# Leaving out 50 of the 125 idle matrix products among the first attention units

## The chip, the cores and the metric

The kernel runs on one core of one Trainium2 chip. The metric is the time of one execution on the device in microseconds (us). The engines are PE (TensorE, matrix products; PEld is its weight load), DVE (VectorE), ACT (ScalarE), POOL (GpSimd) and SP (SyncE, which issues transfers). Each takes its own instructions strictly in the order in which the program has them, and waits at one until what that one needs is there.

## The reference

A recurrent attention (4 batches, 8 heads, 768 steps, head size 48) gives 3072 tokens of width 384. Two expert layers follow: a dense one with a gated activation and a layer norm, and one that sends each token to one of 8 experts.

```
for t in range(S):                         # attention, per batch and head
    cur   = (u * k[t]) outer v[t]
    y[t]  = r[t] @ (state + cur)
    state = w[t][:, None] * state + k[t] outer v[t]
h  = x @ w_in                              # first layer, 3072 x 1024
ln = layernorm(h * softmax(h)) * g_ln
x2 = ln @ w_out
e  = argmax(x2 @ w_gate)                   # second layer
out = gate * (relu(x2 @ w1[e]) @ w2[e])
```

## The kernel before, in words

The attention is cut into 24 units: 6 chunks of 128 steps for each of 4 batches, all 8 heads at once. For a unit, PE turns w, r and k with its transposes (L686, tiles lw, lr, lk); DVE makes running products of the decay (L700, tile qe); ACT and POOL make their reciprocals (L710, L712 on ACT; L717, L721, L722 on POOL, tile tq); DVE forms kt (L727) and rt (L705). PE multiplies kt by rt (L762, the scores); DVE copies the masked scores into am (L766); PE forms the unit's output (L780), turns kt back (L795) and forms the state's update (L807, from ks, which ACT copies at L800). ACT and DVE split each output into a high and a low part (L785, L788).

The first 7 units run without any product of the expert layers beside them. In that time the weights of the first layer, which arrive as 64-bit numbers, are also put together with bit operations on DVE (L226 to L229) and split on ACT and POOL, and PE turns the output weights for the gate (L256, L263). This part takes some 81 us of the run. From then on each attention unit is emitted together with a unit of the first layer (products of L186 to L189), and at the end come the 8 experts.

The order of all of this is written down. Every step is entered in a plan with a planned time by `at(t, fn)`. `emit` sorts the plan by that time and then calls the steps in the order of a fixed list of 2000 numbers, `_ORDER`. So a step keeps its place as long as the number of steps and their planned times stay as they are.

The idle products are eight such steps. `WARM` holds pairs of a count and a planned time, and each pair becomes one step that issues that many products of a 128x128 block of ones with itself, in bfloat16, into a corner of a PSUM bank that nobody reads:

```
WARM = (28, -213.38, 17, 35.27, 40, -60.18, 7, -131.3, 21, 14.69, 0, 23.63, 11, 143.22, 1, 178.42)

def warm(n):
    for _ in range(n):
        nc.tensor.matmul(flat(0)[:, DM:512], ones16, ones16, start=True, stop=True)

for n, t in zip(WARM[0::2], WARM[1::2]):
    at(min(t, t_step[LAG] - 2.0), lambda n=n: warm(n))
```

The planned times are numbers of the plan and no times of the chip. One of the eight counts is 0 already: such a step stands in the plan and issues nothing.

Of the kernel before, what the change touches and what calls it, by code (L numbers as in the profile page):

```python
# [119 lines left out]
def rwkv_moe_kernel(ctx: ExitStack, tc: tile.TileContext, r, k, v, w, u, w_in, w_out, g_ln, w_gate, w1, w2, out, dbg=None):  # L120
# [480 lines left out]
    def at(t, fn):  # L601
        plan.append((t, len(plan), fn))
# [60 lines left out]
    }  # L663
    TAIL0 = 4.0
    STEP = {'po': 56.09, 'pi': 84.42, 'mix': 15.94, 'last': 19.69, 'tail': 8.58}
    WARM = (28, -213.38, 17, 35.27, 40, -60.18, 7, -131.3, 21, 14.69, 0, 23.63, 11, 143.22, 1, 178.42)
    mode_of = lambda s: "po" if s < 3 else "pi" if s < LAG else "mix" if s < NU - 1 else "last" if s == NU - 1 else "tail"
    t_step = {-1: 0.0}
    for s in range(-1, NU + LAG + 2):
# [411 lines left out]
# [6 lines that stand above are left out]
# [306 lines left out]
```

## Time and profile before

| what | us |
|---|---|
| median of 3 runs | 651.63 |
| lowest, highest of the 3 | 649.35, 655.84 |
| the profiled execution | 653.84 |
| its span, first to last instruction | 651.8 |
| PE busy in the span | 617.9 |

The mean granted clock of PE over the span is 0.981 of full speed. An execution's time is 2.0 us longer than its span. The profiled execution is one of several and lies 2.2 us above the median, within what the three runs span.

### The profile page before, as it was taken

How to read it: one execution, taken by the hardware profiler on the slowest of the kernel's cores; microseconds unless marked ns; L12 is line 12 of the kernel's file. 1: busy time of each engine (PE TensorE's matmuls, PEld its weight loads, DVE VectorE, ACT ScalarE, POOL GpSimd, SP SyncE). 2: the span in 40 equal slices, each digit the busy share in tenths (PEclk: the TensorE clock that was granted, in tenths of full speed). 3: DMA queues.
4: the chain of work that ended last, by engine and by line, in shares of the span. 5: the costliest groups of instructions: out<-in, count | busy, mean ns of one | idle time of the engine just before them, and what ended most of it. 6: DMA issues, size and time to landing. Idle time of an engine off the chain costs nothing. (4 is left out here: it accounts for less than half of the span.)

```text
span 651.8 us, 13454 instructions
## 1 busy us (share of the span) xinstructions
PE 617.9 (95%) x5143; PEld 562.8 (86%) x5143; DVE 355.0 (54%) x876; ACT 340.2 (52%) x711; POOL 369.0 (57%) x389
## 2 busy tenths in 40 slices
PE   5888899999999999999999999899999999999993
PEld 4767688888898888888888998898999999999993
DVE  8999967685767767868657675233212112121210
ACT  5577655564755646554547874245354335353420
POOL 7998896453485635466202344276467546566611
PEclk9789899999999999999999999899999999999997
DMA  8984414436443423511004401554445415535200
GB/s 210 239 215 115 99 20 87 114 106 189 135 117 67 99 50 74 103 34 38 13 1 121 147 25 50 194 180 143 145 142 195 153 56 179 168 113 184 73 34 26
DMA packets 125103, 72.56 MB, mean 111 GB/s; under 512 B 104071, under 2 KB 115836, under 8 KB 125029
## 3 DMA queue, kind: packets, MB, share of 16 engines
q1 hardware_dynamic: 121749, 62.13, 35.3%
q0 software_dynamic: 3280, 9.47, 3.9%
q8 instruction: 43, 0.70, 0.5%
q14 instruction: 31, 0.25, 0.1%
HBM read 55.79 MB, written 16.29 MB: 111 GB/s over the span
## 5 line engine op out<-in xcount | busy, mean ns | idle before, releaser
L1254 DVE SCALAR_TENSOR_TENSOR hl<-bank,hh 128x384 fp32r<-128x384 f32 (+5 forms) x70 | 37.0, 551 | 113.3 <-ACT hh L1253 103.8
L1047 POOL TENSOR_TENSOR wbl<-stg,wbh 128x768 fp32r<-128x768 f32 x32 | 58.8, 1852 | 27.7 <-ACT wbh L1046 25.5
L1253 ACT ACTIVATE hh<-bank 128x384 fp32r<-128x384 f32 (+5 forms) x70 | 33.0, 489 | 78.4 <-PE bank L189 63.8
L195 PE MATMUL bank<-wbh,hh 128*128 128x384 f32 (+4 forms) x216 | 73.9, 342 | 0.0
L195 PE MATMUL bank<-wbl,hh 128*128 128x384 f32 (+4 forms) x216 | 72.6, 336 | 0.0
L186 PE MATMUL bank<-xth,wah 128*128 128x384 f32 (+5 forms) x210 | 71.3, 344 | 0.6 <-ACT xth L1246 0.5
L187 PE MATMUL bank<-xtl,wah 128*128 128x384 f32 (+5 forms) x210 | 70.1, 339 | 0.2 <-DVE xtl L1247 0.2
L1047 POOL TENSOR_TENSOR wal<-stg,wah 128x1024 fp32r<-128x1024 f32 x24 | 57.4, 2402 | 20.9 <-ACT wah L1046 18.9
L186 PE MATMUL bank<-wbh,lh 128*128 128x392 f32 x192 | 67.7, 353 | 0.5 <-ACT hh L1253 0.5
L187 PE MATMUL bank<-wbl,lh 128*128 128x392 f32 x192 | 65.3, 340 | 0.0
L1273 POOL DMA_INDIRECT out_dram<-yo,xg x28 | 27.6, 985 | 58.2 <-ACT yo L1270 40.7
L717 POOL TENSOR_TENSOR tq<-qe,yq 128x512 f32<-128x512 f32 x24 | 29.9, 1244 | 51.0 <-ACT yq L712 39.1
L189 PE MATMUL bank<-xth,wal 128*128 128x384 f32 (+5 forms) x210 | 48.1, 338 | 0.0
L958 POOL DMA_INDIRECT xsd<-xo,ai x24 | 24.4, 1017 | 40.1 <-DMA xsd<-xo,ai 16.6
L395 DVE TENSOR_TENSOR ll<-bank,lh 128x512 fp32r<-128x512 f32 x48 | 32.6, 685 | 22.7 <-ACT lh L391 20.3
L186 PE MATMUL pair<-wah,wah 128*128 128x512 f32 x102 | 41.4, 406 | 1.2 <-DVE wbl L268 0.9
L195 PE MATMUL bank<-wbh,hl 128*128 128x384 f32 (+4 forms) x216 | 42.1, 336 | 0.0
L186 PEld LDWEIGHTS bank<-xth,wah 128*128 128x128 f32 x210 | 40.2, 191 | 2.2 <-ACT xth L1246 0.6
L187 PEld LDWEIGHTS bank<-xtl,wah 128*128 128x128 f32 x210 | 40.3, 192 | 1.4 <-DVE xtl L1247 0.4
L358 ACT ACTIVATE cc<-s,nmu 128x1024 f32<-128x1024 f32 x24 | 27.6, 1151 | 26.3 <-DVE nmu L356 25.6
L195 PEld LDWEIGHTS bank<-wbh,hh 128*128 128x128 f32 (+4 forms) x216 | 39.3, 182 | 0.9
L195 PEld LDWEIGHTS bank<-wbl,hh 128*128 128x128 f32 (+4 forms) x216 | 39.4, 182 | 0.8
(236 smaller groups left out, 1635.8 us busy)
## 6 DMA issues: line engine op xcount, KB each, us to landing
stg<-in_moe_w_dram SPq DMA_DIRECT2D x32, 384.0 KB, 3.1
stg<-in_moe_w_dram SPq DMA_DIRECT2D x24, 512.0 KB, 4.2
xsd<-zrow SPq DMA_DIRECT2D x16, 386.0 KB, 5.8
xg<-xsd SPq DMA_DIRECT2D x24, 193.0 KB, 3.1
lw<-in_w_dram SPq DMA_DIRECT2D x24, 192.0 KB, 3.8
lr<-in_r_dram SPq DMA_DIRECT2D x24, 192.0 KB, 4.2
lk<-in_k_dram SPq DMA_DIRECT2D x24, 192.0 KB, 2.9
lv<-in_v_dram SPq DMA_DIRECT2D x24, 192.0 KB, 2.6
```

Of the source, the lines that this page charges most:

```text
L186: nc.tensor.matmul(o, ah, bh, start=(i == 0), stop=False)
L187: nc.tensor.matmul(o, ah, bl, start=False, stop=False)
L189: nc.tensor.matmul(o, al, bh, start=False, stop=(i == n - 1))
L195: nc.tensor.matmul(o, a, b, start=(i == 0), stop=(i == len(seq) - 1))
L358: nc.scalar.activation(out=u["cc"], in_=u["s"], func=AF.Identity, bias=u["nmu"])
L395: yield 1.05 + 0.55 * g, lambda g=g, gs=gs: nc.vector.tensor_tensor(out=u["ll"][:, gs, :], in0=lp[g], in1=u["lh"][:, gs, :].bitcast(F32), ...
L717: nc.gpsimd.tensor_tensor(out=u["tq"], in0=u["qe"][:, :, 1:129], in1=u["yq"], op=ALU.mult)
L958: nc.gpsimd.indirect_dma_start(out=xsd, out_offset=bass.IndirectOffsetOnAxis(ap=u["ai"][:, j, :], axis=0), in_=MU[m]["xo"], in_offset=None ...
L1047: at(t + c1, lambda: eng.tensor_tensor(out=dl(), in0=u["st"], in1=dh().bitcast(F32), op=ALU.subtract))
L1253: at(t + d1, lambda: nc.scalar.activation(out=P2["h", 0][:, f, cs], in_=hp, func=AF.Relu))
L1254: at(t + d2, lambda: nc.vector.scalar_tensor_tensor(out=P2["h", 1][:, f, cs], in0=hp, scalar=0.0, in1=P2["h", 0][:, f, cs].bitcast(F32), o ...
L1273: nc.gpsimd.indirect_dma_start(out=out, out_offset=bass.IndirectOffsetOnAxis(ap=xg(j, i)[0:n, XW - 1:XW].bitcast(I32), axis=0), in_=box["y ...
```

## The change

Four of the eight counts are set to 0: those of 17, 21, 11 and 1 products. The groups of 28, 40 and 7, which are issued together at the start, stay.

```
-    WARM = (28, -213.38, 17, 35.27, 40, -60.18, 7, -131.3, 21, 14.69, 0, 23.63, 11, 143.22, 1, 178.42)
+    WARM = (28, -213.38, 0, 35.27, 40, -60.18, 7, -131.3, 0, 14.69, 0, 23.63, 0, 143.22, 0, 178.42)
```

The number of steps and their planned times are as before, so all other instructions keep their order. Without the idle products the list of PE's instructions is the same in both programs, and so are those of DVE, ACT, POOL and SP.

On PE, before, the group of 17 stands between a state update (L807) and the scores of a unit (L762). The sixteen further pairs of a weight load and a product are not shown:

```order
L795 MATMUL bank_160<-ident,kt 128x128 x4
L686 MATMUL bank_159<-ident,lw_165 128x128 x4
L256 MATMUL pair_158<-ident,wst 128x128 x6
L807 MATMUL bank_160<-lv_175,ks 64x48 x8
L1084 LDWEIGHTS ones_78
L1084 MATMUL pair_158<-ones_78 128x128
```

On PE, after, the scores follow the state update directly (bank_161 and bank_162 are the PSUM banks of the even and odd heads' scores):

```order
L795 MATMUL bank_160<-ident,kt 128x128 x4
L686 MATMUL bank_159<-ident,lw_165 128x128 x4
L256 MATMUL pair_158<-ident,wst 128x128 x6
L807 MATMUL bank_160<-lv_175,ks 64x48 x8
L762 MATMUL bank_161<-rt,kt 128x128
L762 MATMUL bank_162<-rt,kt 128x128
```

Nothing else moved here: the 34 rows are gone. The same holds at the single product, on PE some way further on, where the next instruction is a transpose of r:

```order
 L256 MATMUL pair_158<-ident,wst 128x128 x3
 L807 MATMUL bank_160<-lv_176,ks 64x48 x8
-L1084 LDWEIGHTS ones_78
-L1084 MATMUL pair_158<-ones_78 128x128
 L686 MATMUL bank_163<-ident,lr_169 128x128 x4
 L263 MATMUL pair_158<-wgt,wT 128x8 x3
```

The weight load and the product are gone, and the neighbours keep their places.

## Rows read from the trace of the kernel before

**Rows 1.** Busy time of each engine in two stretches (windows view).

```profile
core 0: us, PE busy (x) PEld busy (x) DVE busy (x) ACT busy (x) POOL busy (x), PEclk, DMA share, GB/s
3.55:81.00 77.45, 62.41 (x846) 53.54 (x846) 71.28 (x126) 52.84 (x126) 68.64 (x68) 0.91 0.76 180
81.00:641.00 560.00, 555.44 (x4298) 509.22 (x4298) 281.13 (x737) 285.62 (x585) 296.48 (x288) 1.00 0.35 104
```

**Rows 2.** The idle products of L1084: shortest, median, longest ns.

```profile
L1084 PE MATMUL pair<-ones x125: 216/219/314, 4.4 to 71.0; 128*128 128x128 bf16 x125
```

**Rows 3.** Timeline of PE: start, us, what, [idle before <- releaser].

```profile
20.32 1.35 PE L1084 MATMUL pair<-ones 128*128 128x128 bf16 x21
23.46 1.10 PE L807 MATMUL bank<-lv,ks 128*64 128x48 f32 x16 [1.80 <-ACT ks L800]
...
30.93 1.12 PE L1084 MATMUL pair<-ones 128*128 128x128 bf16 x17
31.98 1.16 PE L762 MATMUL bank<-rt,kt 48*128 48x128 f32 x16
```

**Rows 4.** Timeline of ACT at 21.7 to 23.4 us.

```profile
21.71 0.72 ACT L710 ACTIVATE yq<-qe,tiny 128x512 f32<-128x512 f32 x1 [4.35 <-POOL tq L722]
...
22.84 0.56 ACT L800 COPY ks<-bank 128x512 f32<-128x512 f32 x1
```

**Rows 5.** Timeline of DVE: all its rows with a wait from 18 to 77 us.

```profile
18.58 1.36 DVE L700 TENSOR_TENSOR_SCAN qe<-bank,zeros 128x128 f32<-128x128 f32 x4 [0.35 <-PE bank L686]
...
33.18 0.76 DVE L766 COPY_PREDICATED am<-causal,bank 128x512 f32<-128x512 int32 x1 [0.37 <-PE bank L762]
...
38.98 0.69 DVE L727 TENSOR_TENSOR kt<-bank,tq 128x512 f32<-128x512 f32 x1 [0.25 <-POOL tq L722]
...
47.69 1.37 DVE L700 TENSOR_TENSOR_SCAN qe<-bank,zeros 128x128 f32<-128x128 f32 x4 [0.82 <-PE bank L686]
...
55.97 1.38 DVE L766 COPY_PREDICATED am<-causal,bank 128x512 f32<-128x512 int32 x2 [0.57 <-PE bank L762]
...
76.53 1.37 DVE L766 COPY_PREDICATED am<-causal,bank 128x512 f32<-128x512 int32 x2 [0.82 <-PE bank L762]
```

**Rows 6.** Timeline of POOL: two rows with a wait, neighbours among its waits.

```profile
27.14 1.37 POOL L717 TENSOR_TENSOR tq<-qe,yq 128x512 f32<-128x512 f32 x1 [0.37 <-DVE kt L727]
...
51.55 1.45 POOL L717 TENSOR_TENSOR tq<-qe,yq 128x512 f32<-128x512 f32 x1 [1.36 <-ACT yq L712]
```

**Rows 7.** Timeline of PE, 60 to 81 us.

```profile
60.12 0.78 PE L1084 MATMUL pair<-ones 128*128 128x128 bf16 x11
...
63.45 0.66 PE L686 MATMUL bank<-ident,lr 128*128 128x128 f32 x4 [0.60 <-DVE rt L705]
...
73.10 0.66 PE L795 MATMUL bank<-ident,kt 128*128 128x128 f32 x4 [0.89 <-DVE su L815]
...
74.54 1.97 PE L762 MATMUL bank<-rt,kt 48*128 48x128 f32 x16 [0.35 <-DVE wal L788]
...
80.98 0.50 PE L186 MATMUL pair<-wah,wah 128*128 128x512 f32 x1 [0.91 <-DVE wbl L268]
```

**Rows 8.** Windows view by granted clock (PEclk, before the last two columns).

```profile
16.67:20.08 3.41, 3.41 (x24) 3.08 (x24) 2.77 (x8) 0.69 (x3) 3.41 (x4) 0.50 1.14 250
20.08:23.49 3.41, 1.61 (x29) 1.32 (x25) 3.28 (x5) 1.78 (x4) 3.33 (x4) 1.00 1.05 242
23.49:26.91 3.42, 3.42 (x48) 2.91 (x52) 3.32 (x5) 2.41 (x7) 3.13 (x4) 0.50 0.95 275
26.91:43.97 17.06, 13.65 (x199) 11.17 (x195) 16.30 (x33) 12.85 (x31) 16.11 (x17) 1.00 0.87 208
43.97:47.39 3.42, 3.42 (x28) 3.04 (x28) 2.90 (x4) 2.42 (x6) 3.25 (x4) 0.50 1.15 238
...
74.69:78.10 3.41, 3.41 (x44) 3.05 (x48) 2.59 (x4) 1.76 (x5) 3.41 (x4) 0.50 1.10 220
...
419.40:422.90 3.50, 3.48 (x16) 3.48 (x17) 0.00 (x0) 1.84 (x3) 1.19 (x1) 0.51 0.90 308
```

## The prediction

> **What bounds the kernel now.** I read the busy time by stretches first [rows 1]. From 81 to 641 us PE is busy 555.44 of 560 us at a granted clock of 1.00: here every microsecond that PE starts later ends the kernel later. From 3.55 to 81 us PE is busy only 62.41 of 77.45 us, DVE 71.28 and POOL 68.64. In this first part PE has slack, and DVE and POOL with their order of work set when the dense part can begin. The idle products all lie in it: the 125 of L1084 have a median of 219 ns each, and the last one starts at 71.0 us [rows 2]. The dense part begins at 80.98 us, when PE, after 0.91 us of waiting, gets what DVE made last (L268) [rows 7]. So the question is whether leaving out 50 products changes when DVE and POOL are done with the first part. Two ways lead there: PE's place in their waits, and PE's clock.
>
> **The change part by part: the time of the products.** Nothing else moves on any engine, so what can go is what the four groups take from PE. The 21 start at 20.32 and take 1.35 us. The 17 start at 30.93, and the scores behind them at 31.98: 1.05 us [rows 3]. The 11 take at most 0.78 us [rows 7], the single one at most 0.22 us [rows 2]. Together at most 3.4 us of PE.
>
> The 21: behind them PE sits idle for 1.80 us all the same, until ACT has copied ks at 23.40 [rows 3, 4]. ACT was late because it had waited 4.35 us, until 21.71, for POOL [rows 4]. Without the products the pause is longer and ends at the same moment. Value: 0.
>
> The 17: this is the group that somebody waits for. The scores end at 31.98 + 1.16 = 33.14, and DVE, idle for 0.37 us, starts its masked copy at 33.18 [rows 3, 5]. Without the group the scores can begin about 1.05 us earlier and DVE loses its wait. What is late next is POOL: DVE's next wait, 0.25 us at 38.98, ends with POOL's L722 [rows 5], and POOL has no wait between the two at 27.14 and 51.55 [rows 6], so it runs through without needing anything sooner. DVE's 0.37 us will come back as a wait of about 0.62 us at 38.98. Value: 0. The bound below is -0.37 us, if POOL too were helped by DVE's earlier work.
>
> The 11 and the single one: DVE has no wait between 55.97 and 76.53 [rows 5], so PE is not what it lacks there; PE itself waits 0.60 us for DVE's rt at 63.45 [rows 7]. Value: 0. For the single product I take 0 as well; the bound is its 0.22 us.
>
> **The clock.** Before, the granted clock was 0.50, which is the 1.2 GHz level, in four stretches of the first part and in one later, at 419.4 [rows 8]. Ahead of the stretch that begins at 23.49 PE had been busy for 1.61 of 3.41 us, with the 21 products among that: the group did not keep the clock up. Ahead of the one at 43.97 lay 17.06 us at full clock, of which PE was busy 13.65 us [rows 8], with the 17 early in it.
>
> What does a slow stretch cost? The same 16 products of L762 take 1.16 us at full clock [rows 3] and 1.97 us at half [rows 7]. What reaches the end is less, since PE has slack here. I take it from the waits of DVE for PE inside or right behind each stretch: 0.35 us at 18.58, none for the stretch at 23.49, 0.82 us at 47.69, 0.82 us at 76.53 [rows 5]. That is 1.99 us for four, 0.5 us each and at most 0.82. In the dense part there is no slack: PE was busy 3.48 us at 0.51 [rows 8], and half of that, 1.74 us, is the price of that stretch.
>
> The Trainium skill, "TensorE: Matmul & The Clock Gate", section "Terms", prices the time at the lower clock at that time multiplied by one minus the clock's ratio, here one half. By it the four stretches (13.66 us together) would cost 6.8 us, where DVE's waits show 1.99; in the dense part the rule and the row agree.
>
> How many stretches will there be without the 50? The 21 products were in vain, so there nothing changes. Around the 17 the pause of PE grows by what the scores move forward, less than 0.4 us in this first look: about 1.05 us earlier at the front, and the masked copy only 0.37 us earlier behind. Around the 11 the pause before 63.45 grows by at most 0.78 us. That makes at most 1.4 us, and less than the 1.80 us behind which the clock was low at 23.49 [rows 3, 8]. I expect the same number of slow stretches, perhaps shifted, and take 0; the bounds are one stretch fewer (-0.82) and one more in the dense part (+1.74).
>
> **The sum** against the profiled execution: 0 + 0 + 0 + 0 for the groups and 0 for the clock, 653.84 us as before, between -1.4 (-0.37 - 0.22 - 0.82) and +1.74 us. That execution is 2.2 us above the median of 651.63, a difference as large as any term here. I forecast the median unchanged, 651.6. Within 1% (6.5 us) is about what a measurement of this kernel can tell from no change.
>
> **Rivals.** First, faster: the products stood on the path after all, because the waits that the trace names are only those that ended last. Then all of their 3.4 us come back: 651.6 - 3.4 = 648.2. For it speaks DVE's 0.37 us at 33.18; against it the three other groups, behind which PE goes on waiting for others.
>
> Second, slower, by the clock. Without the groups of 17 and 11 the clock falls in more places of the first part, and each fall makes DVE wait for PE as at 47.69 and 76.53. Three more stretches at 0.82 us, and one that reaches over 81 us into the dense part at 1.74 us, make 4.2 us: 655.8. It decides where PE at half clock becomes what DVE waits for, which a unit's scores do: 1.97 instead of 1.16 us. For it speaks that four stretches were slow even with the products; against it that PE, once slow, is busy all the time (3.41 of 3.41 us) and the clock rose after each [rows 8], so that a fall does not stay.
>
> The Trainium skill's page "TensorE: Matmul & The Clock Gate", section "Why this matters for your kernels", warns against pauses of PE between bursts of products, since the clock then goes back to half: it speaks against this change. The trace agrees that it fell after pauses (behind the 1.80 us at 23.46), and shows that idle products in front of one did not prevent it. By the price of half the slow time that the Trainium skill gives, four more stretches would be 6.8 us and the time 658.4.
>
> Third, a different length of the stretch at 419.4, or none, by chance: 1.74 us either way, as executions differ anyway (649.35 to 655.84); this is part of the forecast's own spread.
>
> **How the numbers follow.** Forecast 0.70, first rival 0.12, second 0.18. The forecast's own range is the sum's bounds and the spread of the three runs, about 649 to 655. With the first rival at 648.2 and the second at 655.8 partly in, the range is 648.8 to 655.6. Faster by more than 1% (below 645.1) is more than all 50 products are worth: 0.02. Slower by more than 1% (above 658.1) needs eight further stretches at 0.82, or the second rival with two more falls in the dense part: 0.05. Within 1%: 0.93.
>
> **What the changed profile would show.** If I am right: the wait of DVE for L762 near 33.18 is gone, and that of DVE for POOL's L722 near 38.98 has grown to about 0.6 us; PE's wait for ks near 23.46 has grown from 1.80 to about 3.1 us; the dense part begins within 1 us of 80.98; the stretches at clock 0.50 are four or five before 81 us. I am wrong on the slow side if there are seven or more such stretches and DVE's waits for PE add up to over 5 us; on the fast side if the dense part begins before 79 us at the same clock.

## The result, and the profile after

| | before | after |
|---|---|---|
| median of 20 runs each, us | 652.52 | 656.94 |
| lowest, highest | 649.35, 658.51 | 654.92, 659.48 |
| the profiled execution, us | 653.84 | 658.72 |
| its span, us | 651.8 | 656.9 |
| mean granted clock of PE in it | 0.981 | 0.970 |

The kernel became slower: the ratio is 1.0064 with a 95% interval of 1.0048 to 1.008, some 4.2 us. That is less than 1%, and outside the forecast range. The instructions of all engines are the same but for the 50 products, so the time must lie in when things run. The windows view of the profile after, for the two stretches of [rows 1]:

```profile
3.55:81.00 77.45, 64.12 (x756) 55.19 (x759) 69.05 (x123) 51.70 (x123) 67.17 (x67) 0.82 0.73 176
81.00:641.00 560.00, 553.42 (x4321) 507.15 (x4313) 283.65 (x740) 285.68 (x585) 297.21 (x289) 0.99 0.36 104
```

In the first part PE is busy longer (64.12 us for 62.41) with 90 products fewer in the stretch (the 50, and others that now come after 81 us), and the granted clock has gone from 0.91 to 0.82. DVE and POOL got less done in it (69.05 for 71.28, 67.17 for 68.64): they waited. Where the clock is low shows in the windows view cut at its changes, to be held against [rows 8]:

```profile
16.08:19.49 3.41, 3.32 (x16) 2.99 (x18) 2.33 (x6) 1.29 (x5) 3.33 (x4) 0.50 0.99 201
19.49:22.91 3.42, 0.85 (x16) 0.66 (x12) 3.29 (x7) 1.11 (x2) 3.34 (x4) 1.00 1.09 244
22.91:39.98 17.07, 15.86 (x146) 13.02 (x147) 14.77 (x25) 11.50 (x30) 13.55 (x16) 0.50 0.70 181
39.98:46.80 6.82, 5.61 (x86) 4.76 (x88) 6.19 (x14) 4.61 (x11) 6.59 (x7) 1.00 0.96 222
46.80:50.21 3.41, 3.41 (x30) 3.02 (x19) 2.74 (x4) 2.72 (x7) 3.24 (x4) 0.50 1.01 224
422.27:429.10 6.83, 6.37 (x30) 5.96 (x30) 1.26 (x3) 3.22 (x5) 3.78 (x2) 0.50 0.68 224
```

Where before had 3.42 us at 0.50 from 23.49 and then 17.06 us at 1.00, after has 17.07 us at 0.50, though PE is busy in 15.86 of them. The timeline of PE, rows that answer to [rows 3, 7] and two more:

```profile
23.55 1.10 PE L807 MATMUL bank<-lv,ks 128*64 128x48 f32 x16 [3.21 <-ACT ks L800]
...
28.80 1.09 PE L795 MATMUL bank<-ident,kt 128*128 128x128 f32 x4
29.68 1.06 PE L686 MATMUL bank<-ident,lw 128*128 128x128 f32 x4
30.54 0.85 PE L256 MATMUL pair<-ident,wst 128*128 128x128 f32 x3
31.95 0.90 PE L256 MATMUL pair<-ident,wst 128*128 128x128 f32 x3 [0.57 <-ACT wT L259]
32.78 1.10 PE L807 MATMUL bank<-lv,ks 128*64 128x48 f32 x16
33.81 2.08 PE L762 MATMUL bank<-rt,kt 48*128 48x128 f32 x16
...
83.67 0.50 PE L186 MATMUL pair<-wah,wah 128*128 128x512 f32 x1 [0.93 <-DVE wbl L268]
...
420.90 0.55 PE L1244 MATMUL bank<-ident,xg 128*128 128x128 f32 x3 [2.63 <-DMA xg<-xsd]
```

The pause before ks ends at 23.55 (23.46 before), as it should without the 21. But the scores that began at 31.98 with the 17 products ahead of them begin at 33.81 without, and take 2.08 us instead of 1.16. The engines behind them, in the timelines of DVE, ACT and POOL (one fence, the same profile):

```profile
35.92 0.76 DVE L766 COPY_PREDICATED am<-causal,bank 128x512 f32<-128x512 int32 x1 [1.93 <-PE bank L762]
41.83 0.69 DVE L727 TENSOR_TENSOR kt<-bank,tq 128x512 f32<-128x512 f32 x1 [0.63 <-PE bank L686]
...
34.01 0.48 ACT L813 COPY su<-bank 128x384 f32<-128x384 f32 x1 [2.11 <-PE bank L807]
...
34.56 1.09 POOL L820 TENSOR_TENSOR St<-su,qe 64x192 f32<-64x192 f32 x2 [2.51 <-ACT su L813]
```

DVE's wait of 0.37 us at 33.18 [rows 5] has become 1.93 us at 35.92; POOL, which had no wait between 27.14 and 51.55 [rows 6], now waits 2.51 us for ACT, which waited 2.11 us for PE's L807. From 44 us on the first part is late by the same amount. Matching PE's instructions of the two traces one by one (start after minus start before): +0.15 us at 27, +2.66 at 44, +2.65 at 53, +2.68 where the dense part begins (83.67 for 80.98, worked out at its first rows), +2.19 at 412, +4.92 from 425 to the end. So there are **two places**: some 2.5 us arise between 27 and 44 us, about 0.5 us is regained in the dense part, and 2.73 us arise between 412 and 425 us, where the experts start. These figures belong to this pair of profiles, and profiles of one kernel differ (below).

At the second place PE waits for the rows gathered for the first expert: 2.63 us at 420.90 in after. In the profile before the same wait reads as follows (timeline of PE, not shown so far):

```profile
417.10 1.15 PE L1244 MATMUL bank<-ident,xg 128*128 128x128 f32 x6 [1.03 <-DMA xg<-xsd]
```

The gather is issued by SP, which waits for the last scatter of rows. SP's waits from 405 to 424 us, first after, then before:

```profile
SPq L1235 <- DMA xsd<-xo,ai: 4.1, 1, 4.1
```

```profile
SPq L1235 <- DMA xsd<-xo,ai: 2.3, 1, 2.3
```

The pause is 1.60 us longer, and behind it PE is busy 6.37 us at clock 0.50 where it was 3.48 before [rows 8]; half of that difference is 1.45 us. Together 3.05, of which 2.73 show in the starts.

### The profile page after: what moved, and what is told of

The parts are those of the page before. It is cut to its first block, busy times and chain, and to the rows that moved or that the text cites. A ratio compares the mean times of both kernels' runs of the same rounds, so it can differ in the third digit from the quotient of the medians.

```text
span 656.9 us, 13354 instructions
## 1 busy us (share of the span) xinstructions
PE 622.3 (95%) x5093; PEld 566.8 (86%) x5093; DVE 355.3 (54%) x876; ACT 339.8 (52%) x711; POOL 369.2 (56%) x389
## 5 line engine op out<-in xcount | busy, mean ns | idle before, releaser
L1047 POOL TENSOR_TENSOR wal<-stg,wah 128x1024 fp32r<-128x1024 f32 x24 | 57.2, 2397 | 22.0 <-ACT wah L1046 19.6
L717 POOL TENSOR_TENSOR tq<-qe,yq 128x512 f32<-128x512 f32 x24 | 30.1, 1254 | 50.1 <-ACT yq L712 35.3
L358 ACT ACTIVATE cc<-s,nmu 128x1024 f32<-128x1024 f32 x24 | 27.6, 1151 | 25.5 <-DVE nmu L356 25.4
L195 PEld LDWEIGHTS bank<-wbh,hh 128*128 128x128 f32 (+4 forms) x216 | 39.3, 182 | 0.9
```

The source lines that it names most:

```text
L195: nc.tensor.matmul(o, a, b, start=(i == 0), stop=(i == len(seq) - 1))
L358: nc.scalar.activation(out=u["cc"], in_=u["s"], func=AF.Identity, bias=u["nmu"])
L717: nc.gpsimd.tensor_tensor(out=u["tq"], in0=u["qe"][:, :, 1:129], in1=u["yq"], op=ALU.mult)
L1047: at(t + c1, lambda: eng.tensor_tensor(out=dl(), in0=u["st"], in1=dh().bitcast(F32), op=ALU.subtract))
```

## The experiments

Every kernel was compared with the kernel before on the same chip. The table has the ratio (95% interval) and what one profile of each shows: where the clock was 0.50, for stretches that begin between 13 and 45 us; the start of DVE's third masked copy of L766 (33.18 before); the first row of the dense part (80.98 before); PE's pause before the first gathered rows, near 417 us, and the time at 0.50 behind it (1.03 and 3.4 before). "None" stands for a pause that is no longer there; "ahead" for half clock that is over before this pause (410.9 to 414.3 us in no17, 409.8 to 413.2 in no11, behind another pause of 2.18 and 2.35 us). Each profile is one execution, and single executions differ. With "21" stand the kernels that issue 21 or more full products at 20 us.

| kernel | ratio | at 0.50, us | copy | dense | pause, 0.50 |
|---|---|---|---|---|---|
| before (21) | 1 | 16.7–20.1, 23.5–26.9, 44.0–47.4 | 33.18 | 80.98 | 1.03, 3.4 |
| look_before (21) | | 14.3–21.1 | 32.85 | 80.62 | 0.86, 0 |
| only21 (21) | 1.0022 (0.9998–1.0047) | 15.4–22.2, 35.8–39.3 | 32.84 | 79.76 | 1.16, 3.4 |
| no17 (21) | 1.0024 (0.9998–1.005) | 15.0–21.8, 35.4–42.3 | 32.84 | 81.83 | 1.25, 3.4 ahead |
| no11 (21) | 1.0025 (1.0005–1.0046) | 13.8–20.7 | 32.83 | 80.55 | 0.14, 3.4 ahead |
| one48 (21) | 1.0007 (0.9983–1.003) | 15.8–19.2, 36.2–39.7 | 32.83 | 79.75 | 0.63, 3.4 |
| fill21 (21) | 1.0014 (0.9992–1.0037) | 15.7–19.1, 29.3–32.7, 43.0–46.4 | 34.07 | 82.16 | 0.68, 0 |
| moved_with (21) | 1.0013 (0.999–1.0037) | 16.2–19.6, 36.7–40.1 | 32.87 | 82.51 | 0.68, 0 |
| late_with (21) | 0.9998 (0.9974–1.0022) | 15.7–19.1, 29.3–32.7, 43.0–49.8 | 34.08 | 81.35 | none, 0 |
| swap_with (21) | 0.999 (0.9969–1.001) | 16.1–19.5, 36.5–40.0, 43.4–46.8 | 32.83 | 82.38 | 0.42, 0 |
| both_with (21) | 1.0024 (0.9999–1.0049) | 16.1–19.5, 36.6–40.0, 43.4–46.8 | 32.86 | 82.47 | none, 0 |
| fillboth (21) | 1.0048 (1.0027–1.007) | 25.4–35.6 | 36.36 | 81.88 | 2.43, 6.8 |
| after | 1.0064 (1.0048–1.008) | 16.1–19.5, 22.9–40.0 | 35.92 | 83.67 | 2.63, 6.8 |
| look_after | | 15.1–39.0 | 35.91 | 82.22 | 2.73, 6.8 |
| no21 | 1.0057 (1.004–1.0075) | 14.7–35.2 | 36.70 | 84.50 | 1.30, 3.4 |
| tiny21 | 1.0028 (0.9999–1.0056) | 16.1–19.5, 22.9–36.5 | 37.30 | 82.84 | 2.69, 3.4 |
| moved_without | 1.0042 (1.0019–1.0064) | 14.9–35.3 | 34.75 | 82.36 | 2.69, 6.8 |
| late_without | 1.0036 (1.0017–1.0055) | 14.4–28.0, 38.3–41.7 | 34.63 | 81.76 | 1.45, 0 |
| swap_without | 1.0036 (1.001–1.0063) | 16.8–20.2, 23.6–27.0, 44.1–47.5 | 32.74 | 81.01 | 0.92, 3.4 |
| both_without | 1.0043 (1.0023–1.0063) | 16.6–20.0, 23.4–26.8, 43.9–47.3 | 32.73 | 81.46 | 0.08, 3.4 |

Two things hold over the whole table. First, in all runs and not only in the profiles, every kernel with the 21 has a higher mean granted clock (0.981 to 0.985) than every kernel without (0.973 to 0.978; 10 to 20 runs each). Second, matched to the profile of before, the profiles without the 21 are on average later than those with them by 1.1 us just behind the dense part's start (85 us), by 1.6 us at 405 and by 3.3 us at 425. So about half of the loss arises ahead of the experts' start and half there.

**The theory** after the result: without the 21 products PE's clock is at half when PE starts again behind the pause before ks, and stays there through the row of PE's work from 27 to 35 us on which DVE and POOL wait. **Its rivals**: the 17 or the 11, not the 21, carry the time; the products' place in PE's order matters and not their work; or the whole loss arises at the start of the experts.

### Which group carries the time

The edits are in the table of counts alone, against the kernel before.

```diff
-    WARM = (28, -213.38, 17, 35.27, 40, -60.18, 7, -131.3, 21, 14.69, 0, 23.63, 11, 143.22, 1, 178.42)
no21:
+    WARM = (28, -213.38, 17, 35.27, 40, -60.18, 7, -131.3, 0, 14.69, 0, 23.63, 11, 143.22, 1, 178.42)
only21:
+    WARM = (28, -213.38, 0, 35.27, 40, -60.18, 7, -131.3, 21, 14.69, 0, 23.63, 0, 143.22, 0, 178.42)
no17:
+    WARM = (28, -213.38, 0, 35.27, 40, -60.18, 7, -131.3, 21, 14.69, 0, 23.63, 11, 143.22, 1, 178.42)
no11:
+    WARM = (28, -213.38, 17, 35.27, 40, -60.18, 7, -131.3, 21, 14.69, 0, 23.63, 0, 143.22, 0, 178.42)
```

no11 leaves out the single product together with the 11, though its expectation names the 11 alone.

> Only the 21 products are left out; 17, 11 and 1 stay. Theory A (the 21 products are what lets PE's clock rise again behind the stretch that begins near 23 us; without them it stays at half to about 40 us): as slow as the changed kernel, +3 to +5 us, ratio 1.005 to 1.008, and PE's dense part begins 2 to 3 us later than 81. Theory B (the 17 products hold the clock): no change, 0 to +0.5 us. Theory C (each group carries a part): +1 to +2 us.

> The 21 products stay; 17, 11 and 1 are left out. Theory A: as the kernel before, within 0.5 us, dense part at 81. Theory B: +3 to +5 us. Theory C: +2 to +3 us. If the excess of the changed kernel lies in the late gather near 417 us and has nothing to do with the products, both this and the run without the 21 show the same time.

> Only the 17 products are left out. Theory A: 0, within 0.5 us; DVE's wait for the scores near 33.2 us is gone and its wait for POOL near 39 us grows to about 0.6 us. Theory B: +3 to +5 us. Theory C: +1 to +2 us.

> Only the 11 products near 60 us are left out. Theories A and B: 0, within 0.5 us. Theory C: +0.5 to +1.5 us, through a slow stretch between 61 and 64 us that DVE's wait for PE there would show.

Leaving out the 21 alone gives 1.0057, nearly the whole loss; leaving out the other three groups and keeping the 21 gives 1.0022. The means of the two kernels' runs lie 2.3 us apart, with a 95% interval of 1.6 us to either side. The windows view of no21, at half clock and behind it, and DVE's masked copy in its timeline:

```profile
14.73:35.21 20.48, 15.94 (x130) 13.60 (x131) 17.76 (x30) 10.69 (x28) 17.12 (x18) 0.50 0.87 215
35.21:40.00 4.79, 3.53 (x62) 2.77 (x59) 3.30 (x6) 4.29 (x11) 3.47 (x4) 1.00 0.63 168
```

```profile
36.70 0.76 DVE L766 COPY_PREDICATED am<-causal,bank 128x512 f32<-128x512 int32 x1 [2.73 <-PE bank L762]
```

The windows view of only21, and the same copy there:

```profile
15.36:22.19 6.83, 6.02 (x41) 5.47 (x41) 5.64 (x11) 2.41 (x8) 6.67 (x7) 0.50 1.03 238
22.19:35.84 13.65, 9.00 (x139) 7.29 (x137) 13.49 (x23) 11.68 (x29) 12.81 (x14) 1.00 0.87 219
35.84:39.25 3.41, 3.16 (x26) 2.75 (x27) 2.90 (x6) 0.85 (x4) 3.24 (x4) 0.50 1.10 217
```

```profile
32.84 0.72 DVE L766 COPY_PREDICATED am<-causal,bank 128x512 f32<-128x512 int32 x1
```

With the 21 the clock is back at 22.19, before the pause ends, and DVE does not wait for the scores at all; without them it stays at half until 35.21 and DVE waits 2.73 us. The three smaller groups: no17, no11 and only21 lie at 1.0022 to 1.0025, some 1.5 us. Theory A had expected no change beyond 0.5 us for each; the intervals of no17 and only21 include 1, that of no11 (from 1.0005) just does not, so a small part for these groups (theory C) is not excluded. What the 17 do may show in the profiles: the three kernels of this table that have the 21 (or 48) but not the 17 (only21, no17, one48) have a half-clock stretch that begins at 35 to 36 us; no11 and look_before, with the 17, have none there. But moved_with, swap_with and both_with have the 17 and a stretch at 36.5, so this is a hint and no proof. For the 11 no profile shows a role. The parts don't add exactly (3.7 us for the 21 and 1.5 for the rest, against 4.2), and the intervals are wide enough for that.

### The same two kernels profiled again

> The changed kernel once more, one look: is the long half-clock stretch in its first part there again? Theory A: yes, 10 us or more between 14 and 40 us, and the dense part begins 2 to 4 us later than in a look at the kernel before.

> The kernel before once more, one look. Theory A: the half-clock stretches are over by 27 us and none lies between 27 and 34 us; the dense part begins at 79.5 to 81 us.

No edit. look_after repeats what the first profile of after showed: half clock from 15.12 to 39.01 us, the copy at 35.91 with the wait of 1.93 us, the pause of 2.73. It also has one more stretch of 3.4 us at half clock, at 284.8 us in the dense part, which no other profile has; its lag against before grows there from 1.19 to 3.22 us. look_before does not repeat the profile that the prediction was read from. Its windows view and its group of 21 in the timeline of PE:

```profile
14.27:21.10 6.83, 4.91 (x30) 4.36 (x31) 5.63 (x11) 3.12 (x9) 6.67 (x7) 0.50 0.86 202
21.10:24.51 3.41, 2.18 (x40) 1.95 (x39) 3.38 (x5) 2.68 (x6) 3.34 (x3) 1.00 1.04 276
```

```profile
20.96 1.40 PE L1084 MATMUL pair<-ones 128*128 128x128 bf16 x21
```

Here the scores of the unit ahead are slow, the 21 products run from 20.96 to 22.36, the clock rises at 21.10, among them, and there is no fall behind the pause: the next half clock is at 72.3 us. Of the twelve profiles of kernels with the 21 (or 48), ten are like this one in the point that counts: the clock stays at 1.00 from the pause until 29 us or later. Only the first profile of before (from 23.50) and fillboth (from 25.36) fell before 27 us. Of the eight profiles without (tiny21, below, among them), all eight were at half when PE started again at 23.5 or fell there, and five stayed at half all the way from 27 to 35 us. What PE did before sorts them too: its pause ahead of ks is 2.20 to 3.21 us in the eight and in fillboth, and 0.58 to 2.12 us in the others, among them before with 1.80, the one of these that fell.

### Work or place

The 21 products stay in their place, but with 8 columns in both operands instead of 128; tiny21 has all other groups.

```diff
         for _ in range(n):
+            if n == 21:
+                nc.tensor.matmul(flat(0)[0:8, DM:DM + 8], ones16[:, 0:8], ones16[:, 0:8], start=True, stop=True)
+                continue
             nc.tensor.matmul(flat(0)[:, DM:512], ones16, ones16, start=True, stop=True)
```

> The 21 products keep their place and number, but each is 8 columns by 8 instead of 128 by 128, so PE has nearly no work from them. Theory A (the work of the 21 products brings the clock back): as without them, +3 to +4 us, ratio about 1.0055, a stretch at half clock of 10 us or more before 36 us. Theory D (the 21 act by their place or number as instructions, with the clock a bystander): as the kernel before, within 0.5 us.

Timeline of PE, DVE's masked copy, and the windows view of tiny21:

```profile
20.25 0.67 PE L1085 MATMUL pair<-ones 128*8 128x8 bf16 x21
23.55 0.67 PE L807 MATMUL bank<-lv,ks 128*64 128x48 f32 x8 [2.63 <-ACT ks L800]
```

```profile
37.30 0.75 DVE L766 COPY_PREDICATED am<-causal,bank 128x512 f32<-128x512 int32 x1 [3.30 <-PE bank L762]
```

```profile
22.88:36.53 13.65, 12.41 (x111) 10.50 (x113) 10.84 (x18) 8.28 (x22) 10.38 (x12) 0.50 0.67 171
```

The profile is that of after: half clock from 22.88 to 36.53 and a wait of 3.30 us. By the time the case is weaker: 1.0028 lies between the kernel before and no21, and its runs spread from 650.67 to 659.88 us, wider than those of no21 (654.13 to 658.49). The clock of all its runs decides more: a mean of 0.977, among the kernels without the 21 (0.973 to 0.978) and below all with them (0.981 to 0.985). Small products in the same place do not keep the clock up as the full ones do; how much of the time they save is not shown.

### More idle products

fill21 and one48 have 48 products where the 21 stand, which fills the pause before ks but for 0.63 and 0.58 us; one48 has no other of the four groups. fillboth also fills the pause ahead, from 12.6 to 16.2 us.

```diff
fill21, fillboth:
+    WARM = (28, -213.38, 17, 35.27, 40, -60.18, 7, -131.3, 48, 14.69, 0, 23.63, 11, 143.22, 1, 178.42)
one48:
+    WARM = (28, -213.38, 0, 35.27, 40, -60.18, 7, -131.3, 48, 14.69, 0, 23.63, 0, 143.22, 0, 178.42)
fillboth:
-        at(o("Tk"), lambda: transposes(lk[sl], kb))
+        def tk():
+            if i == 1:
+                warm(55)
+            transposes(lk[sl], kb)
+        at(o("Tk"), tk)
```

> 48 products in place of the 21, all else as before: they fill the pause of PE up to 23.4 us. Theory A: the clock no longer falls at 23.5 us, or rises sooner; DVE hardly waited for PE in that stretch, so -1 to 0 us. If the 48 end too late for the copied ks they cost up to +0.3 us.

> 48 products in place of the 21; the 17, 11 and 1 left out. Theory A: as the run that keeps only the 21 or better, +0 to +1.5 us: what the smaller groups add comes from the later falls near 36 and 72 us.

> As the run with 48, and 55 further products in PE's pause from 12.6 to 16.2 us, in front of a unit's transposes of k. Theory A: the clock stays at full speed from the start to about 36 us; DVE's wait of 0.35 us for PE at 18.6 us goes: -1.5 to -0.3 us. If what a slow stretch costs is only what DVE's waits showed, no more than -0.4 us.

fill21 and one48 can't be told from the kernel before (1.0014 and 1.0007). one48 has none of the groups of 17, 11 and 1, and no loss is seen; that the longer group makes up for them is not shown, since only21 can't be told from one48. fillboth was expected to be faster than before and was slower, 1.0048. Its timeline of PE, windows view and DVE's masked copy (line numbers are 4 higher there):

```profile
18.74 2.85 PE L1088 MATMUL pair<-ones 128*128 128x128 bf16 x48
23.80 0.67 PE L811 MATMUL bank<-lv,ks 128*64 128x48 f32 x16 [2.20 <-ACT ks L804]
```

```profile
25.36:35.60 10.24, 9.67 (x88) 8.27 (x78) 6.86 (x14) 6.08 (x16) 7.83 (x10) 0.50 0.70 169
```

```profile
36.36 0.76 DVE L770 COPY_PREDICATED am<-causal,bank 128x512 f32<-128x512 int32 x1 [4.10 <-PE bank L766]
```

The clock did stay up from 12 to 25 us, and then it fell for 10.24 us in the very place where DVE needs PE. The second pause was not filled, though: the work ahead of it ran at full clock and was done sooner, the 48 products ended at 21.59 us, and 2.20 us of pause were left, more than the 1.80 of before. All its half clock before 81 us is 13.65 us, as much as before has (13.66, [rows 8]), and the dense part begins at 81.88 for 80.98: what the place of the slow time is worth in this pair is 0.90 us at most. The rest of the some 3 us (1.0048) is not located; this profile also has a pause of 2.43 us and 6.8 us at half clock at the experts' start.

### Less work in the stretch that waits

The transposes of L256 that stand between 28 and 33 us (with their wait for ACT's copy L259) are emitted behind the scores of the same unit, so that the scores come sooner; once with all 125 products, once without the 50.

```diff
                     nc.tensor.matmul(sc[q][:, p, :], u["kt"][rows, p, :], u["rt"][rows, p, :], start=True, stop=True)
+            if i == 1:
+                gate_step(1)
         at(o("scores"), scores)
...
-                named(lambda f=c: prep_gate(f, wst(f), wgt, scratch(f), wtp, gp), d("t", "w", "l"))
+                for n, tt in enumerate(d("t", "w", "l")):
+                    at(tt, lambda f=c, n=n: gate_step(f) if (f, n) not in LATER else None)
```

(`gate_step(f)` calls the next step of the gate's preparation for weight block f; two further steps are called likewise behind L766 and L780 of that unit.)

> All idle products as before; two groups of three transposes for the gate (L256) that stood ahead of the scores near 29 and 30 us, and ACT's copy between them, are issued behind these scores instead. Theory E (the price of the half clock is PE's row of work between 27 and 34 us, which reaches DVE's masked copy and POOL's update of the state; elsewhere the half clock costs little): PE was not late there at full clock, so 0, within 0.7 us of the kernel before.

> The same move with the 17, 21, 11 and 1 products left out. In the changed kernel these transposes with PE's wait between them took 2.2 us (30.5 to 32.8). Theory E: DVE's wait for the scores (1.93 us) and POOL's for the copy of the update (2.51 us) go although the clock is still at half; the dense part begins at 81 to 82 us, the time is within +1.5 us of the kernel before, ratio under 1.0025. If a half clock costs as such, or the loss arises elsewhere: still +4 us, 1.006.

1.0013 with the products, 1.0042 without. In the profile of moved_without the clock is at half from 14.86 to 35.34, and the scores begin at 31.69 (timeline of PE, lines 1 to 10 higher) instead of 33.81:

```profile
30.66 1.10 PE L817 MATMUL bank<-lv,ks 128*64 128x48 f32 x16
31.69 2.08 PE L763 MATMUL bank<-rt,kt 48*128 48x128 f32 x16
33.70 0.90 PE L256 MATMUL pair<-ident,wst 128*128 128x128 f32 x3
```

PE's lag against the kernel before is 1.35 us at 53 us instead of 2.65, so the cut in PE's row of work does halve the first part of the loss in the profile, as the theory asks. Against its own partner nothing is left of it: the dense part begins at 82.36 in moved_without and at 82.51 in moved_with, which has no half clock between 27 and 35 us. The time did not follow as far as expected (at most 1.0025), which is a miss: at the second place this profile has the pause of 2.69 us and 6.8 us at half clock, as after has.

### The start of the experts

Three pairs of kernels, each with and without the 50. late_*: idle products in the pause before the gathered rows. swap_*: a weight load of 512 KB that is issued shortly behind the last scatter (0.76 us in before, 0.17 in after) goes behind the gathers instead. both_*: the two together.

```diff
late, both:
         def tr():
+            if j == 0 and i == 2:
+                idle(20)
             for kk in range(KD):
                 nc.tensor.transpose(xp[:, kk, :], xg(j, i)[0:n, kk * 128:(kk + 1) * 128], ident[0:n, 0:n])
+            if j == 0 and i == 3:
+                idle(8)
swap, both:
-        at(t, load)
+        at(t, (lambda: held.append(load)) if late else load)
...
+            if (j, i) == (0, 3):
+                for load in held:
+                    load()
```

> All idle products as before, and 20 more in PE's pause near 416 us (PE waits for the gathered rows of the experts' first tiles) and 8 behind the transposes that follow it. Theory F (about 2 us of the loss of 4.4 arise there: a longer pause, and behind it a longer half clock at 1.75 us per 3.4 us of stretch): the half clock behind the pause is gone or shorter, -0.5 to -1.5 us against the kernel before. If the pause is not what lowers the clock there: 0 to +0.5.

> The same 28 products at the experts' start, and the 17, 21, 11 and 1 left out. Theory F: the long half clock behind the pause shrinks, +2 to +3 us against the kernel before instead of +4.4. If the loss all arises in the first 81 us: +3.5 to +4.5 still.

> All idle products as before; one 512 KB load of the second expert's weights is issued behind the gathers of two tiles instead of ahead of them. In looks at the kernel before the last scatter was ahead of that load anyway: 0, within 0.7 us.

> The same order of transfers with the 17, 21, 11 and 1 left out. Theory G (in the changed kernel the last scatter comes to lie behind that load, which makes the pause 2.6 instead of 1.0 us): the wait for the scatter falls from 4.0 to about 2.1 us, the pause to about 1 us, and the time to +2 to +3 us against the kernel before. If something else delays the scatter: the pause stays above 2 us, +4 us.

> All idle products as before, the 28 products at the experts' start and the load behind the gathers together. If pause and half clock near 417 us cost the kernel before about 1 us on average: -0.5 to -1.5 us, ratio 0.998 to 0.999; if they cost it nothing: 0.

> The same with the 17, 21, 11 and 1 left out. Theory F with G: what remains of the loss against the run with them is the part of the first 81 us alone, 2 to 2.7 us; ratio 1.001 to 1.003 against the kernel before. If the late part has nothing to do with it: +4 us between the two.

Against after's 1.0064 the three kernels without the 50 stand at 1.0036 (late, swap) and 1.0043 (both), and the half clock behind the pause is 0 (late_without) and 3.4 us (the other two) instead of 6.8. So part of the loss seems to be had at this place alone; the intervals of all three overlap that of after. Between the kernels of a pair the 50 products are worth 0.0038 (late), 0.0046 (swap) and 0.0019 (both), against 0.0064 unchanged; with intervals of about 0.002 on each ratio these three can't be told from each other. both_with was expected 0.5 to 1.5 us under the kernel before and was at 1.0024, both_without at 1.001 to 1.003 and was at 1.0043: two misses, and no version of this study is clearly faster than the kernel before.

One profile here speaks against a simple form of the theory. The windows view of swap_without, which has no idle product at 20 us:

```profile
20.17:23.59 3.42, 0.34 (x8) 0.14 (x8) 3.29 (x5) 1.87 (x4) 3.34 (x4) 1.00 1.02 238
23.59:27.00 3.41, 3.41 (x52) 2.85 (x52) 3.31 (x6) 2.33 (x7) 3.06 (x4) 0.50 0.94 284
27.00:35.00 8.00, 6.21 (x84) 4.94 (x76) 7.77 (x16) 6.28 (x16) 7.52 (x8) 1.00 0.80 194
```

PE was busy for only 0.34 us before the fall at 23.59, and the clock rose again at 27.00, as in the first profile of before. both_without did the same, and in both the dense part begins within 0.5 us of 80.98, so that what these two profiles can tell of the loss of 1.0036 and 1.0043 lies behind it. In these two and in before the half clock began only as the pause ended; in after, look_after, no21, tiny21 and moved_without PE was at half already while it paused, and there the clock stayed low past 35 us; late_without too was at half in the pause and rose at 28.02. So leaving out the 21 makes a half clock through 27 to 35 us likely and not certain: five profiles of eight, and two of the five whose first part is just that of after (after and look_after; not late_without, swap_without and both_without).

## Why the prediction was wrong

**The time of the products: right.** The four groups' own time was worth 0. The pause before ks ends at 23.55 as before, with a wait of 3.21 us where about 3.1 was forecast; nothing came back of the 3.4 us, and the first rival (648.2) is out. The fairest test is swap_without, whose first part is that of after with the clock's course of before. Two rows of its timeline of DVE, to be held against [rows 5]:

```profile
32.74 0.73 DVE L766 COPY_PREDICATED am<-causal,bank 128x512 f32<-128x512 int32 x1
...
38.99 0.69 DVE L727 TENSOR_TENSOR kt<-bank,tq 128x512 f32<-128x512 f32 x1 [0.25 <-POOL tq L722]
```

DVE's 0.37 us for the scores is gone as predicted, nothing is gained by 38.99, and the dense part begins at 81.01. One particular was wrong: the wait for POOL stays at 0.25 us and does not grow to 0.6, because DVE's lead is used up before: it waits 0.19 us for ACT at 33.66 and makes kt at 34.61 as in before. (At full clock the 0.37 us is gone with the 17 in place too: look_before has the copy at 32.85 without a wait.) In after itself the signs failed with the clock: a longer wait for the scores, no wait for POOL near 38.98, and a dense part that begins 2.69 us later and not within 1 us.

**The clock: the step that failed** is "The 21 products were in vain, so there nothing changes … I expect the same number of slow stretches, perhaps shifted, and take 0". It rested on one execution, in which the clock fell at 23.49 although the 21 stood there. That was the exception: ten of twelve profiles with the products have no fall there, and without them all eight are at half at 23.5 or from there. The term of 0 for the clock should have been a loss: after has 27.3 us at half clock ahead of its dense part for the 13.66 of before, 6.8 for 3.4 at the experts' start, and a mean clock over all its runs of 0.973 for 0.983. The experiments no21 and only21 give the price: 1.0057 without the 21, 1.0022 with them and without the rest. The rows to distrust were [rows 8]: a fall after a group proves that the group did not prevent it this time, not that it never does.

The second rival had the size (655.8, +4.2 us) and the kind, a lower clock. Two of its particulars were wrong. It counted more short stretches at 0.82 us each; what came is as many stretches before 81 us as before had, four (the last at 77.5), of which one is 17.07 us long. In the profiles with such a long stretch (after, look_after, no21, tiny21) the lag is 2.46 to 3.00 us at 53 us. So the count of four or five stretches came out as forecast and said nothing, since their length had doubled; of the two signs for the slow side, seven stretches did not come, and DVE's waits for PE did pass 5 us (5.3 us in the first 85 us, 3.0 before). And the argument against it, "that PE, once slow, is busy all the time … so that a fall does not stay", fell: in 22.91 to 39.98 PE was busy 15.86 of 17.07 us and the clock stayed. The Trainium skill's warning against pauses before bursts ("TensorE: Matmul & The Clock Gate", "Why this matters for your kernels") had the right sign here.

**The price of slow time** was taken as an average of 0.5 us per stretch of 3.4 us in the first part, and on average that is what the profiles show: over the twenty, the dense part begins 0.14 us later for each us at half clock ahead of it (6.8 to 27.3 us; correlation 0.74), 0.47 us per stretch. Single profiles lie up to 1.6 us off that line. The amount of slow time was mis-sized, and not its price. That its place counts more than its sum, as fillboth could suggest, is not shown: the time at half between 27 and 35 us goes with the dense part's start less closely (0.64). From 27 to 35 us PE's chain L795, L686, L256, its wait for ACT, L256, L807, L762 leads to waits of DVE and POOL, which the rows of after show; but in no17, with the clock at half from 35.4 to 42.3 us instead, the lag against before goes from -0.39 us at 35 us to +2.36 at 44. That the stretch from 27 to 35 us carries the time of every run is argued from single profiles.

**The dense part.** The price of 1.74 us for a stretch at half there was no measurement, but half of a row's busy time taken as lost; the profiles bear it out: from the dense part's first row to the end the profiles without half clock between 409 and 430 us take 568.2 to 570.4 us, those with 3.4 us 570.0 to 572.6, those with 6.8 us 571.7 to 574.4 (the last is look_after, with its further stretch at 284.8). What the prediction held for chance (the third rival) went with the change: of the profiles of kernels that are not edited at this place, the pause is 2.4 to 2.7 us in four of five without the full 21 products (after, look_after, tiny21, moved_without) and in one of nine with them (fillboth), and 1.30 or less in the others. What goes with it is the last scatter. Where SP issues the 512 KB load 0.74 to 1.36 us behind it (nine profiles, both of before among them), the scatter has landed 3.1 to 3.7 us after its issue; where the load follows after 0.12 to 0.36 us (after, look_after, tiny21, moved_without, late_without, no17), its packets go first and the scatter takes 4.5 to 4.7 us; with the load moved away (swap, both) it takes 2.75 to 2.91. So the load delays the scatter. Why it follows so closely when the first part is late is **open**, and two profiles do not fit: no17 has the late scatter with a pause of only 1.25 us, behind the earlier pause of 2.18, and fillboth the long pause with a scatter of 3.4 us.

**The clock over all runs.** In 148 runs of the kernel before the mean granted clock lies between 0.975 and 0.990 (mean 0.983), and the time falls by 5.3 us for each 0.01 of it (correlation -0.81). The 20 runs of after have a mean of 0.973. That difference of 0.010 would be 5.3 us, and 4.2 were measured: the clock is enough to account for the whole loss, if the time hangs on it as that line has it, though it does not say in which place.

## What to carry to other kernels

Idle products are worth the slow time that they prevent behind the next pause, at the price that slow time has there: in this kernel about half of it in the dense part, where PE is the limit, and on average 0.14 us per us ahead of it. Read the clock from several executions before calling a group useless, since one execution shows one of several courses; the mean clock of all runs told the kernels with the 21 from those without, where single profiles overlapped. And filling more is not safer: with 103 products in two pauses the work between them was done sooner, a pause of 2.20 us came back behind them, and the kernel was slower than before.

## What the runs showed of the hardware that was not expected

The granted clock can stay at 0.50 for 10 to 24 us while PE is busy most of the time: 15.86 of 17.07 us in after, 9.67 of 10.24 in fillboth, half clock from 15.12 to 39.01 in look_after. In look_before it rose at 21.10 behind a stretch of 6.83 us in which PE was busy for 4.91. What makes it rise is not settled by these runs. A fall also came after long full work: in fillboth the clock had been up from before 12 us, with 103 products in the two pauses, and it fell at 25.36, behind a pause of 2.20 us, for longer than the falls of before.
